# Causal attention and a mixture of experts on one core: half blocks of keys in 64 by 64 tiles, and six transfers let go one by one

## The chip, the core and the metric

The kernel runs on one core of a Trainium2 chip. The metric is the device time of one execution in microseconds; the median of the executions shown stands for the kernel.

## The reference

Eight batches of 576 tokens, eight heads of 64, then eight experts of which each token takes one:

```python
scores = q @ k.T / sqrt(64)                       # causal
cum = cumsum(max(s, 0))
scores = where(causal, -1e9, scores + min(cum_j - cum_i, 0))
x = softmax(scores) @ v                           # (B, H, S, D) -> (B, S, H*D)
logits, local = x @ w_gate, sigmoid(x @ w_local)
e = argmax(logits), or the previous token's e where local >= 0.5 and s > 0
out = softmax(logits)[e] * (relu(x @ w1[e]) @ w2[e])
```

All is in fp32. Each fp32 matmul of the program stands as two records (two passes) in the profile.

## The kernel before, in words

**Attention.** Two heads form a pair `n`; there are 32 pairs (four per batch), and two pairs form a slot `m`, so there are 16 slots. The bias of the reference is a factor of the key: `weigh(n)` multiplies the values of a pair, and a column of ones, by key weights `wk` into one of four buffers `vg`, so that the same product gives the sum of the softmax in a further column. A row of `vg` has 64 + 2 columns per head.

Keys lie in blocks of 128 (`c` = 0 to 3; `c` = 4, `NF`, holds the last 64, loaded as the last 128 keys with the first half weighted zero). Queries lie in blocks of 64 (`j` = 0 to 8).

`scores(n, u)` does one of four units: for every key block of `UNITS[u]` and for both heads one matmul, keys times queries, on tiles of 64 rows by 128 columns; the two heads lie on different rows, so they run at the same time. A unit fills a pair of banks of PSUM (`ps`, one bank per head). One exp on ACT (`L905`) takes the whole unit to `e`; then GpSimd zeroes what lies above the diagonal (`masked`, `L890`). The unit list decides how many columns are computed; for the 64 queries at the head of a 128-key block, the upper half of the keys is masked away again.

`values(n, j0, j1)` sums over the key blocks for each `j`: `e` is the stationary operand (128 keys by 64 queries), `vg` streams 66 columns (`L934`, tiles of 128 rows by 64 columns, the two heads side by side). It fills one bank for `j` below `NJA` = 6 and one for the rest; DVE takes the reciprocal of the sums (`L941`) and multiplies (`L942`) into `xb`. `turn` transposes for the gate product.

The order is written by hand; each engine runs its queue in that order. A slot is: four units of the first pair, four of the second, values of the first, values of the second, `turns` and `weigh` for later pairs. The pool `ps_s` is a ring of three bank pairs, of which each unit takes the next; `ps_o` has the two banks of the values. So a unit waits for the exp three units ahead of it. `plan(slot, place, f)` hangs the routing work on places in a slot (0 and 1 behind the scores of the two pairs, 3 and 4 behind their values, 5 at the end): in slots 4, 8, 12 and 15 the gate product (`product`, `L217`, on tiles of 128 by 32) and its `logits`; two slots later (6, 10, 14) `ranks` (`L301`, `L302`), `rows`, `gates`; then `scatter` of rows to a table in HBM by GpSimd (`L349`). Products and ranks also take bank pairs from the ring.

Transfers are issued by SP. A load that has to follow some work is held back by a copy of one element on ACT (`nc.scalar.copy(kb[0:1, 0:1], behind)`), which reads a result and writes into the tile to be loaded. Before, a slot has two such copies: values `v` of two pairs behind an exp (`L808`), and `k`, `q` of two pairs behind a value product (`L797`).

**Experts.** From 221.6 us on, units of up to 256 tokens go through two layers (`L608`, `L637`), 4 MB of weights for each unit. Nothing of it is changed.

Of the kernel before, what the change touches and what calls it, by code (L numbers as in the profile page):

```python
# [35 lines left out]
NJ = S // DH  # L36
NJA = 6
G1 = 2
REF = (127, 415)
UNITS = (((0, 0, 384, 0),), ((0, 384, S, 0), (3, 384, S, 192)), ((1, P, S, 0),), ((2, 256, S, 0), (NF, TS, S, 320)))  # L40
WIDTH = (384, 384, 448, 384)
GB = 2
# [8 lines left out]
BX = 3  # L51
FIRST = ((0, P, 0, 3 * P), (P, S, 3 * P, S))
CAP = N + DH
# [62 lines left out]
class Router:  # L116
# [104 lines left out]
    def logits(self, g, bs=range(GB)):  # L221
        v = self.nc.vector
        st = self.g[g]
        n, groups = self.columns(bs)
        lt = self.s("lt", [P, NJH, 2, WR])
        v.transpose(lt[:, :n].rearrange("p j q e -> p (j q e)"), st.pop("lp"))
        if "l" not in st:
            st["l"] = self.s("l", [P, NC, E + 1])
        l = st["l"]
        for c, (b, j, skip) in enumerate(groups):  # L230
            for r in range(2):
                v.tensor_copy(l[32 * r : 32 * r + 32, b * NJ + j + skip : b * NJ + j + n],
                              lt[32 * c : 32 * c + 32, skip:n, r, : E + 1])
        c = slice(bs[0] * NJ, bs[-1] * NJ + NJ)
        v.tensor_copy(l[DH:, c], l[:DH, c])

# [529 lines left out]
def attention(ctx, tc, q, k, v, s, wx, ident, recs, wend, router, experts):  # L766
# [9 lines left out]
    p_v = pool("p_v", NVA)  # L776
    p_e = pool("p_e", 2)
    p_x = experts.p_x
    p_x0 = pool("p_x0", 1)
# [6 lines left out]

    ins, vs, es, xs, xts = {}, {}, {}, {}, {}
    heads = [slice(DH * h, DH * h + DH) for h in range(2)]

    def load_qk(n, behind=None):  # L790

        if n >= NPAIR:
            return
        b, hp = divmod(n, HP)
        ins[n] = qb, kb = p_in.tile([P, S], F32, name="qb"), p_in.tile([P, S], F32, name="kb")
        if behind is not None:
            nc.scalar.copy(kb[0:1, 0:1], behind)  # L797
        for k0, k1, q0, q1 in FIRST if n == 0 else ((0, S, 0, S),):
            nc.sync.dma_start(kb[:, k0:k1], k[b][:, hp, k0:k1])  # L799
            nc.sync.dma_start(qb[:, q0:q1], q[b][:, hp, q0:q1])  # L800

# [21 lines left out]
    load_v(1)  # L823
    load_qk(2)
    load_v(2)
    load_qk(3)
    for n in range(3, NVA):
        load_v(n)
    router.projection(wx)
    wk = once.tile([P, NPAIR, G1 + NB, 2], F32, name="wk")  # L830
    nc.gpsimd.memset(wk[:TL, :, G1 + NF], 0.0)
    for t in vgs:
        nc.gpsimd.memset(t[..., VW - 1 : VW], 1.0)
        nc.gpsimd.memset(t[:TL, G1 + NF, :, VW - 1 : VW], 0.0)

# [18 lines left out]
    def key_weights():  # L854
        cps = banks("cps")[:, 0].rearrange("p (i n) -> p i n", n=B * H)
        i = 0
        for w, n in ((w1, G1), (w2, NB)):
            for c in range(n):
                a = min(c * P, S - P)
                tr(cps[:, i], w[:, a : a + P], ident[: B * H, : B * H])  # L860
                i += 1
        for i in range(G1 + NB):
            d = slice(TL if i == G1 + NF else 0, P)
            nc.vector.tensor_copy(wk[d, :, i, :].rearrange("p n h -> p h n"), cps[d, i].rearrange("p (h n) -> p h n", h=2))

# [22 lines left out]

    def masked(ap, n, base=0):
        nc.gpsimd.affine_select(out=ap, in_=ap, compare_op=Alu.is_ge, fill=0.0, base=base, pattern=n,  # L890
                                channel_multiplier=-1)

    def scores(n, u):
        if n >= NPAIR:
            return
        qb, kb = ins[n]
        if u == 0:
            es[n] = [p_e.tile([P, 2, w], F32, name=f"e{i}") for i, w in enumerate(WIDTH)]
        e = es[n][u]
        ps = banks("ps")[:, :, : WIDTH[u]]  # L900
        for c, a, z, at in UNITS[u]:
            key = min(c * P, S - P)
            for h, d in enumerate(heads):
                mm(ps[:, h, at : at + z - a], lhsT=kb[d, key : key + P], rhs=qb[d, a:z], start=True, stop=True)  # L904
        nc.scalar.activation(e, ps, Act.Exp, scale=scale)  # L905
        for c, a, z, at in UNITS[u]:
            m = min(P, z - a)
            if a < c * P + P:
                masked(e[:, :, at : at + m], [[0, 2], [1, m]], P - m)

# [12 lines left out]

    def values(n, j0, j1):
        b, hp = divmod(n, HP)
        if b not in xs:
            xs[b] = x_tile(b) if b < BX else p_x.tile([P, NJ, 2, XW], F32, name="xb")
        xb = xs[b]
        po = ps_o.tile([P, j1 - j0, VW], F32, name=f"po{j0}")
        for j in range(j0, j1):  # L930
            last = j // 2 if j < NJ - 1 else NF
            for c in range(last + 1):
                for h, d in enumerate(heads):
                    mm(po[d, j - j0, :], lhsT=weights_of(n, c, j, h),  # L934
                       rhs=vgs[n % NV][:, c if j < 2 * G1 else G1 + c, h, :],
                       start=(c == 0), stop=(c == last))

        def evacuate():
            m = j1 - j0
            rec = recs[:, n, j0:j1, :]  # L940
            nc.vector.reciprocal(rec, po[:, :, VW - 2 : VW])  # L941
            nc.vector.tensor_tensor(xb[:, j0:j1, :, 32 * hp : 32 * hp + 32], po[:, :, :DH].rearrange("p j (g i) -> p j g i", g=2),  # L942
                                    rec[:, :, 0].unsqueeze(2).unsqueeze(3).to_broadcast([P, m, 2, 32]), op=Alu.mult)

        return evacuate, po[0:1, 0, 0:1]

# [20 lines left out]
    for g in range(NG - 1):  # L967
        m = HP * GB // 2 * (g + 1)
        plan(m, 1, lambda g=g: router.product(g, of(g), banks))
        plan(m, 3, lambda g=g: router.logits(g))  # L970
        plan(m, 5, lambda g=g: (router.codes(g), router.turn1(g)))
        plan(m + 1, 1, lambda g=g: router.exps(g))
        plan(m + 1, 3, lambda g=g: router.turn2(g))
        plan(m + 2, 1, lambda g=g: router.ranks(g, banks))
        plan(m + 2, 3, lambda g=g: router.rows(g))
        plan(m + 2, 3, lambda g=g: router.gates(g, [xs[b] for b in range(g * GB, g * GB + GB)]))
        places = [(m + 2 + i, p) for i, ps in enumerate(STORES[g]) for p in ps]
        for c in range(NC):
            if c >= len(places):
                experts.puts.append(lambda after, g=g, c=c: router.scatter(g, c, after))  # L980
                continue
            i, p = places[c]
            after = {3: (2 * i, NJA), 4: (2 * i + 1, 0), 5: (2 * i + 1, NJA)}.get(p)
            after = after and recs[0:1, after[0], after[1], 0:1]
            plan(i, p, lambda g=g, c=c, after=after: router.scatter(g, c, after))
# [3 lines left out]
    plan(2, 3, range_ends)  # L989
    plan(m - 5, 3, lambda: router.assign_early(0))  # L990
    for i in range(4):
# [3 lines left out]
    plan(m - 1, 1, lambda: router.product(NG - 1, (xts[B - 2],), banks, (0,)))  # L995
    plan(m - 1, 3, lambda: router.logits(NG - 1, (0,)))

    def at(slot, place):
        for f in todo.pop((slot, place), ()):
            f()  # L1000

    for m in range(NPAIR // 2):
        pair = 2 * m, 2 * m + 1
        for n in pair:
            for u in range(len(UNITS)):
                if (n, u) == (0, 2):
                    key_exps()
                scores(n, u)
                if (n, u) == (0, 3):
                    key_weights()  # L1010
                    weigh(0)
                    weigh(1)
                if (n % 2, u) == (1, 1):
                    load_v(n - 1 + NVA, es[n][u][0:1, 0, 0:1])
                    load_v(n + NVA)
            at(m, n - 2 * m)
        for n in pair:
            values(n, 0, NJA)[0]()
            evacuate, done = values(n, NJA, NJ)
            if n % 2 == 0:  # L1020
                load_qk(n + NV, done)
                load_qk(n + 1 + NV)
            evacuate()
            at(m, 3 + n - 2 * m)
        last = m % HP == HP - 1
# [43 lines left out]
def attention_general(ctx, tc, q, k, v, s, w_gate, w_local, cum_d, x_d, ident, lg):  # L1069
# [24 lines left out]
    def load_batch(b):  # L1094
# [6 lines left out]
        nc.sync.dma_start(qb, q[b])  # L1101
        nc.sync.dma_start(kb, k[b])
        for hp in range(HP):
            hs = slice(2 * hp, 2 * hp + 2)
            nc.sync.dma_start(vb[:, :, hs], v[b, hp][:, :NF])
            nc.sync.dma_start(vl[:, hs], v[b, hp][TL:, NF])
        ins[b] = qb, kb, vb, vl
# [500 lines left out]
```

## Time and profile before

| | |
|---|---|
| median of 3 executions | 729.42 us (729.3 to 730.54) |
| the profiled execution, own time | 748.85 us |
| its span | 747.1 us |
| granted TensorE clock | 0.994 |
| attention, up to the first expert matmul | 221.6 us |
| experts | from there to the end |

The profile is of one execution, and its own time is above that of the others; durations and gaps of single steps are read from it, and differences are set against its own order of events. A matmul's end is modelled, so a step is read from start to start: the time from one matmul to the next that follows it on the same tile. PEld is the weight load of TensorE, which overlaps with its matmuls. "Idle before" is time of the engine in front of the named group, and the releaser is what ended it.

### The profile page before, as it was taken

The page shows a single profiled execution, that of the slowest core. Times are in us where ns is not written, and L with a number is a line of the kernel's source. Part 1 is how long each engine was busy: PE and PEld are TensorE (multiplying, and loading weights), DVE is VectorE, ACT ScalarE, POOL GpSimd, SP SyncE. Part 2 cuts the span into 40 slices and gives each one's busy share as a digit, 9 for nine tenths or more (in the row PEclk, how much of TensorE's full clock was granted, in tenths as well). Part 3 has the DMA queues.
Part 4 walks back from the last instruction along what each step waited for, and adds up shares of the span by engine and source line. Part 5 has one row for each costly group of instructions (what it writes and reads, how often), then busy time and mean ns, then how long its engine had stood idle before and what let it go on. Part 6 is the DMA issues. An engine that isn't in the chain of part 4 may idle for free.

```text
span 747.1 us, 16231 instructions
## 1 busy us (share of the span) xinstructions
PE 729.2 (98%) x6537; PEld 504.9 (68%) x6537; DVE 257.7 (34%) x714; ACT 166.0 (22%) x355; POOL 206.7 (28%) x453
## 2 busy tenths in 40 slices
PE   8999999999998999999999999999999999999996
PEld 7888878878876567567567365637644676673675
DVE  4656668677756383101100411041132001104110
ACT  4645454354331011011011010201010111110111
POOL 3543367577574245350100011010101001000100
PEclk9999999999998999999999999999999999999999
DMA  8464455665629996598555979996999965976700
GB/s 303 145 189 149 152 191 165 201 199 172 188 81 382 341 396 218 208 424 240 203 190 169 375 258 396 342 382 237 425 334 390 423 215 214 307 268 239 269 15 32
DMA packets 57205, 187.28 MB, mean 251 GB/s; under 512 B 11837, under 2 KB 32061, under 8 KB 49568
## 3 DMA queue, kind: packets, MB, share of 16 engines
q1 hardware_dynamic: 50224, 165.91, 62.3%
q0 software_dynamic: 6800, 20.09, 7.0%
q8 instruction: 53, 0.87, 0.5%
q14 instruction: 32, 0.26, 0.1%
q10 hardware_dynamic: 96, 0.15, 0.1%
HBM read 165.50 MB, written 20.75 MB: 249 GB/s over the span
## 4 chain that ended last, share of the span: by engine, by line
PE 95%; issue 2%; POOL 1%; DVE 1%; DMA 1%; ACT 0%; SPq 0%; POOLq 0%; ACTq 0%
PE yp L637 34%; PE hp L608 31%; PE po L934 13%; PE ps L904 11%; PE hp L599 4%; PE lp L217 2%; DMA qb<-in_q_dram 1%; POOL table L349 0%; ACT e L905 0%; PE pos L301 0%; POOL e L890 0%; PE pos L302 0%; DVE xb L942 0%; SPq L799 0%; POOL out_dram L641 0%
## 5 line engine op out<-in xcount | busy, mean ns | idle before, releaser
L637 PE MATMUL yp<-w2b,hT 128*128 128x512 f32 (+4 forms) x768 | 258.4, 584 | 0.0
L608 PE MATMUL hp<-xT,w1b 128*128 128x256 f32 (+2 forms) x1216 | 232.0, 352 | 0.0
L608 PEld LDWEIGHTS hp<-xT,w1b 128*128 128x128 f32 x1216 | 207.7, 192 | 30.0 <-issue 7.8
L637 PEld LDWEIGHTS yp<-w2b,hT 128*128 128x128 f32 (+3 forms) x768 | 109.9, 167 | 138.4 <-issue 136.1
L641 POOL DMA_INDIRECT out_dram<-y,gi x37 | 36.4, 984 | 412.3 <-DVE y L639 380.0
L610 ACT ACTIVATE hT<-hp 128x256 f32<-128x256 f32 (+2 forms) x152 | 53.6, 353 | 430.4 <-PE hp L608 417.2
L639 DVE TENSOR_SCALAR y<-yp,gi 128x512 f32<-128x512 f32 (+2 forms) x38 | 27.8, 731 | 299.8 <-PE yp L637 293.4
L934 PE MATMUL po<-vg,e 128*64 128x66 f32 x3200 | 105.2, 223 | 6.9 <-issue 5.6
L934 PEld LDWEIGHTS po<-vg,e 128*64 128x64 f32 x3200 | 98.7, 138 | 13.1 <-issue 10.5
L905 ACT ACTIVATE e<-ps 128x768 f32<-128x768 f32 (+1 forms) x128 | 97.0, 837 | 46.5 <-PE ps L904 45.8
L904 PE MATMUL ps<-qb,kb 64*128 64x192 f32 (+4 forms) x768 | 94.7, 398 | 0.6 <-ACT e L905 0.3
L904 PEld LDWEIGHTS ps<-qb,kb 64*128 64x128 f32 x768 | 64.7, 186 | 29.6 <-ACT e L905 14.9
L890 POOL TENSOR_SCALAR_AFFINE_SELECT e<-e 128x256 f32<-128x256 f32 (+1 forms) x160 | 67.2, 444 | 50.3 <-ACT e L905 49.3
L349 POOL DMA_INDIRECT table<-xb,idx x54 | 54.5, 1009 | 19.6 <-issue 16.8
L619 DVE STREAM_TRANSPOSE hT<-hs 32x256 f32<-32x256 f32 x64 | 27.9, 436 | 78.9 <-ACT hs L601 78.1
L884 DVE TENSOR_TENSOR vg<-va,wk 128x256 f32<-128x256 f32 x64 | 41.5, 714 | 0.0
L941 DVE RECIPROCAL recs<-po 128x12 f32<-128x12 f32 x64 | 13.5, 211 | 64.0 <-PE po L934 45.2
L599 PE MATMUL hp<-w1b,xT 128*32 128x512 f32 (+1 forms) x224 | 28.3, 594 | 0.0
L578 DVE STREAM_TRANSPOSE xT<-xq 128x1024 f32<-128x1024 f32 (+1 forms) x23 | 23.6, 1028 | 11.8 <-DMA xq<-table 11.7
L942 DVE TENSOR_TENSOR xb<-po,recs 128x384 f32<-128x384 f32 (+1 forms) x48 | 22.0, 458 | 2.2 <-POOL xb L325 0.6
L599 PEld LDWEIGHTS hp<-w1b,xT 128*32 128x32 f32 (+1 forms) x224 | 8.1, 114 | 17.8 <-issue 17.8
L953 DVE STREAM_TRANSPOSE xt<-xb 128x576 f32<-128x576 f32 x24 | 17.1, 751 | 0.0
(254 smaller groups left out, 202.6 us busy)
## 6 DMA issues: line engine op xcount, KB each, us to landing
w2b<-in_w_dram SPq DMA_DIRECT2D x30, 2048.0 KB
w1b<-in_w_dram SPq DMA_DIRECT2D x29, 2048.0 KB
va<-in_v_dram SPq DMA_DIRECT2D x32, 320.0 KB
kb<-in_k_dram SPq DMA_DIRECT2D x31, 288.0 KB
qb<-in_q_dram SPq DMA_DIRECT2D x31, 288.0 KB
xq<-table SPq DMA_DIRECT2D x56, 130.0 KB
w1b<-in_w_dram SPq DMA_DIRECT2D x4, 512.0 KB
xq<-table SPq DMA_DIRECT2D x20, 65.0 KB
```

The source lines that it names most:

```text
L349: put = self.nc.gpsimd.indirect_dma_start(out=self.halves, in_=src, element_offset=0, in_offset=None, out_offset=bass.IndirectOffsetOnAxis ...
L599: mm(ps[d, :], lhsT=xT[:, k, d], rhs=self.ws[l][0][:, k, c * 512 : c * 512 + 512], start=(k == 0), stop=(k == DK - 1))
L608: mm(ps[:, :w], lhsT=self.ws[ls[0]][0][:, k, c * P : c * P + P], rhs=xT[:, k, :w], start=(k == 0), stop=(k == DK - 1))
L610: nc.scalar.activation(self.hT[u][:, c, :w], ps[:, :w], Act.Relu)
L619: self.nc.vector.transpose(hT[32 * a : 32 * a + 32, :, 32 * r : 32 * r + 32], hs[32 * r : 32 * r + 32].rearrange("p (c i) -> p c i", i=P)[ ...
L637: mm(ps[d, :], lhsT=hT[:, k, n * P + d.start : n * P + d.stop], rhs=self.ws[l][1][:, k, f : f + w], start=(k == 0), stop=(k == FK - 1))
L641: put = nc.gpsimd.indirect_dma_start(out=self.out[:, :], out_offset=bass.IndirectOffsetOnAxis(ap=gi.bitcast(I32)[:m, n, 0:1], axis=0), in_ ...
L884: nc.vector.tensor_tensor(vg[:, to].rearrange("p c h e -> p (c h) e")[:, :, :DH], va[:, :c].rearrange("p c h e -> p (c h) e"), wk[:, n, to ...
L890: nc.gpsimd.affine_select(out=ap, in_=ap, compare_op=Alu.is_ge, fill=0.0, base=base, pattern=n, channel_multiplier=-1)
L904: mm(ps[:, h, at : at + z - a], lhsT=kb[d, key : key + P], rhs=qb[d, a:z], start=True, stop=True)
L905: nc.scalar.activation(e, ps, Act.Exp, scale=scale)
L934: mm(po[d, j - j0, :], lhsT=weights_of(n, c, j, h), rhs=vgs[n % NV][:, c if j < 2 * G1 else G1 + c, h, :], start=(c == 0), stop=(c == last))
```

## The change

1. **Key order.** The blocks of 64 keys are stored in the order 8, 0, 1, 2, 3, 5, 4, 7, 6 (`BLOCKS`). A 128-key block then starts at the second 64 in storage; the last 64 keys lie at the front.
2. **Three units instead of four.** For each 128-key block the 64 queries at its diagonal that see only half of its keys are left out of `scores`: 512, 384 + 64 and 256 + 128 columns per head, 1344 instead of 1600.
3. **`scores_halves(m)`** computes what was left out: the diagonal blocks 0, 2, 4 and 6 of both pairs of a slot, as 64 by 64 tiles, 16 matmuls of 64 columns in one pair of banks `ph`, one exp of 512 columns and two masks. Blocks 0 and 2 go to one half of the partitions, 4 and 6 to the other. It runs one slot ahead: in slot `m` the halves of slot `m + 1` are done, directly behind the scores (slot 0 does its own too).
4. **`values_halves(n)`** multiplies them with `vg` on 64 by 64 tiles (8 matmuls per pair) into the same sums; `values` has 21 instead of 25 products per head. `NJA` becomes 4, so that the two key halves of a step go to different banks.
5. **Banks.** The values of a slot's second pair (`pb`) and `ph` take bank pairs from the ring of three; the first pair keeps `po`.
6. **Order in a slot:** scores a, scores b, half values a, half scores of the next slot, half values b, values a with evacuation, values b with evacuation.
7. **Transfers.** Six per slot (two `v`, two `k`, two `q`) are let go each behind its own copy, at points named in `POINTS`: behind an exp (`e00` is unit 0 of the first pair), behind the last exp and the half scores (`h`), behind the evacuations of the first pair (`x0`, `x1`). Slot 0 lets go four, slot 1 eight; the last two slots none. Two loads of `v` fewer are issued at the start.
8. **Routing.** Work of place 3 moves to place 1, and the copies of `logits` go from DVE to ACT where both batches are done at once (slots 4, 8, 12).

The core of the diff:

```diff
-UNITS = (((0, 0, 384, 0),), ((0, 384, S, 0), (3, 384, S, 192)), ((1, P, S, 0),), ((2, 256, S, 0), (NF, TS, S, 320)))
-WIDTH = (384, 384, 448, 384)
+BLOCKS = (8, 0, 1, 2, 3, 5, 4, 7, 6)
+UNITS = (((0, DH, S, 0),), ((1, 3 * DH, S, DH), (NF, TS, S, 0)), ((2, 5 * DH, S, 0), (3, 7 * DH, S, 256)))
+WIDTH = (512, 448, 384)
+HALVES = ((0, 4), (2, 6))
+POINTS = {0: ("h", "x0", "x1", "y0"), 1: ("e00", "e10", "e20", "e01", "e11", "h", "x0", "x1"), 2: ("e00", "e20", "e11", "h", "x0", "x1")}
...
+        copy = self.nc.scalar.copy if len(bs) == GB else v.tensor_copy
...
-        for k0, k1, q0, q1 in FIRST if n == 0 else ((0, S, 0, S),):
-            nc.sync.dma_start(kb[:, k0:k1], k[b][:, hp, k0:k1])
-            nc.sync.dma_start(qb[:, q0:q1], q[b][:, hp, q0:q1])
+        todo = [(kb, k, 0, S), (qb, q, 0, S)] if n else [(kb, k, 0, DH + P), (qb, q, 0, FIRST), (qb, q, FIRST, S), (kb, k, DH + P, S)]
+        for to, src, a, z in todo:
+            nc.sync.dma_start(to[:, a:z], src[b][:, hp, a:z])
...
+            for to, of in (heads[:2],) if c == NF else (heads, heads[::-1]) if c in TURNED else ((d, d),):
+                nc.vector.tensor_copy(wk[to, :, i, :].rearrange("p n h -> p h n"),
+                                      cps[of, i].rearrange("p (h n) -> p h n", h=2))
...
+    def scores_halves(m, ps):
+        eh[m] = p_eh.tile([P, 2, 2, len(HALVES), DH], F32, name="eh")
+        ps = ps[:, :, : 4 * DH]
+        for i in range(2):
+            qb, kb = ins[2 * m + i]
+            for t, blocks in enumerate(HALVES):
+                for side, x in zip(heads, blocks):
+                    at = (2 * i + t) * DH
+                    key = BLOCKS.index(x) * DH
+                    for h, d in enumerate(heads):
+                        mm(ps[side, h, at : at + DH], lhsT=kb[d, key : key + DH], rhs=qb[d, x * DH : x * DH + DH],
+                           start=True, stop=True)
+        nc.scalar.activation(eh[m].rearrange("p h n t i -> p h (n t i)"), ps, Act.Exp, scale=scale)
...
+    def values_halves(n, po, first):
+        e = eh[n // 2][:, :, n % 2]
+        for t, blocks in enumerate(HALVES):
+            for part, (side, j) in enumerate(zip(heads, blocks)):
+                for h, d in enumerate(heads):
+                    mm(po[part][d, j - PARTS[part][0], :], lhsT=e[side, h, t],
+                       rhs=vgs[n % NV][side, j // 2 + (G1 if part else 0), h, :],
+                       start=(first > 0 and t == 0), stop=(first == 0 and t == 1))
...
-        for n in pair:
-            values(n, 0, NJA)[0]()
-            evacuate, done = values(n, NJA, NJ)
-            if n % 2 == 0:
-                load_qk(n + NV, done)
-                load_qk(n + 1 + NV)
-            evacuate()
-            at(m, 3 + n - 2 * m)
+        a, b = pair
+        po = room(a)
+        if m == 0:
+            for i in range(2):
+                values(a, po, i, True, False)
+        values_halves(a, po, m)
+        halves = banks("ph") if b + 1 < NPAIR else None
+        to = room(b)
+        scores_halves(m + 1, halves)
+        values_halves(b, to, True)
+        let_go("h", es[b][2][0:1, 0, P : P + 1])
+        for i in range(2):
+            if m:
+                values(a, po, i, False, True)
+            evacuate(a, po, i)
+            let_go(f"x{i}", recs[0:1, a, PARTS[i][0], 0:1])
+        at(m, 3)
+        for i in range(2):
+            values(b, to, i, False, True)
+            evacuate(b, to, i)
+            let_go(f"y{i}", recs[0:1, b, PARTS[i][0], 0:1])
+        at(m, 4)
```

`room(n)` gives `po` for the first pair and `banks("pb")` for the second. `let_go(place, behind)` takes the next of the slot's parts, if the place is one of its points: a one-element ACT copy of `behind` into the tile, then SP's transfer.

## The prediction

> **What bounds the kernel now.** I read the page's busy shares first, then its chain of work that ended last.
>
> ```profile
> PE 729.2 (98%) x6537; PEld 504.9 (68%) x6537; DVE 257.7 (34%) x714; ACT 166.0 (22%) x355; POOL 206.7 (28%) x453
> PE 95%; issue 2%; POOL 1%; DVE 1%; DMA 1%; ACT 0%; SPq 0%; POOLq 0%; ACTq 0%
> ```
>
> TensorE is busy 98% of the span and carries 95% of the chain. The chain in order of time shows the attention stage as slots of two steps without a hole between them:
>
> ```profile
> 43.64 5.76 PE ps L904 x48
> 49.40 5.98 PE po L934 x200
> 55.39 5.76 PE ps L904 x48
> ...
> 210.74 1.46 PE lp L217 x64
> ```
>
> So a slot is 5.76 + 5.98 = 11.74 us of pure TensorE. Behind attention (from 221.6 us on) TensorE runs through the experts without waiting, so a microsecond won in a slot is won at the end. A share would have misled here: ACT is busy 22% of the span, but the table by stretch has it at 6.6 us of this 11.74 us slot, and all eight exps fall into the score half and a little behind it:
>
> ```profile
> 43.57:55.31 11.74, 11.74 (x252) 9.97 (x248) 6.38 (x14) 6.61 (x12) 4.11 (x10) 1.00 0.57 171
> L905 ACT ACTIVATE e<-ps 128x768 f32<-128x768 f32 x96 | 73.0, 812 | 46.5 <-PE ps L904 45.8 <-issue 0.7
> L905 ACT ACTIVATE e<-ps 128x896 f32<-128x896 f32 x32 | 29.2, 914 | 0.0
> ```
>
> Columns of the first line: stretch, its length, then busy us of PE, PEld, DVE, ACT, POOL. The ACT timeline of one slot gives its pace:
>
> ```profile
> 59.24 1.53 ACT L905 ACTIVATE e<-ps 128x768 f32<-128x768 f32 x2
> 60.80 0.19 ACT L808 COPY va<-e 1x1 f32<-1x1 f32 x1
> 60.90 0.90 ACT L905 ACTIVATE e<-ps 128x896 f32<-128x896 f32 x1
> ```
>
> Two exps together take 1.53 us, so the second began at 59.93, 0.69 behind the first. The one-element copy that lets a transfer go reads the exp just issued and waits for its end; the exp behind it starts 0.97 after the one before. **Such a copy costs ACT 0.28 us.**
>
> **What the Trainium skill says.** "TensorEngine Tiling (Array Packing)", Tiling Modes: 64x64 gives four tiles, tiles load and multiply independently, and a change of mode drains the array. The trace agrees on the drain: from the last score matmul to the first value matmul it is 202 ns where a 64-column step takes 56, so 146; back it is 93 plus 107 of bare weight load. It has two- and four-tile steps (64\*128, 128\*64, 128\*32) but no 64\*64 one. The same page, Gotcha 1, wants row tiles in different PSUM banks; the new code does that (heads to banks in the scores, the two parts in the values). "ScalarE: Activation LUTs", What ACT_TABLE_LOAD costs: 186 ns + 0.833 ns a column, overlapping by 93. The rows of 812 and 914 ns sit 10 to 20 ns under it.
>
> **The change part by part**, by start times of matmuls in the clean slot. A step (one pass of all tiles that run together) takes 0.833 ns a column + 3: 163 ns for 192, 376 for 448, 323 for 384, 58.3 for the 66 of the values.
>
> *Removed, scores.* A pair's steps before: 2 x (323 + 163 + 163 + 376 + 270) + 168 (the 64-column piece, one of its two steps waiting for a 128-column weight load of 107) = 2.76 us. After: 2 x (429 + 323 + 216 + 109) + 168 = 2.32. Twice 0.44: 0.87 us a slot.
>
> *Removed, values.* 25 products a head become 21: 100 steps a slot become 84; 16 x 58.3 ns = 0.93.
>
> *Added, half blocks.* 16 score and 16 value matmuls a slot on 64\*64 tiles, each in two passes: 8 + 8 four-tile steps. **Their duration is the unknown.** Lower bound: streaming, 56 and 58. Upper: two tiles at a time, 112 and 117. For the lower speak the L217 row (64 records in 1.46 us with the change of mode; inside, a four-tile step of 96 columns every 83 ns, starts 7 ns apart, so issue isn't the limit) and two row tiles with 107 ns weight loads stepping in 112, hence loading together. I take the lower: 8 x 56 + 8 x 58.3 = 0.92.
>
> *One more change of mode*: 0.15. Without waits: 0.87 + 0.93 - 0.92 - 0.15 = **0.73 us off a slot**.
>
> *What ACT takes back.* Six transfers now have six copies instead of two; three (e00, e20, e11) stand between exps. And ph and pb take two pairs of banks from the ring of three: the built program has ph wait for the exp of b0, and pb for that of b1 (a, b: the slot's pairs; 0 to 2: units). Exps follow at 0.92 (1024 columns, extrapolated), 0.81 and 0.69; one starts 0.27 after its scores' last column (the slot that begins at 55.31: columns end at 56.07, exp at 56.34); TensorE resumes 0.05 after an exp (exp ends at 182.55, scores go on at 182.60). From the slot's first matmul, ACT: a0 1.24; copy; a1 2.44; a2 3.25; copy; b0 4.22; b1 5.14, ending 6.05. TensorE: b1's scores, ready at 3.29, wait for a1's exp until 3.40; scores end 4.86; drain; halves of a 5.01 to 5.24; ph waits until 5.29, ends 5.74; halves of b wait until 6.10, plus 0.05 of bare weight load. Then 0.24 + 0.15 + 4.90 + 0.09: 11.53. Waits 0.52, so **0.21 off a plain slot** (2, 3, 5, 7, 9, 11, 13): 1.5 us. What was TensorE's becomes a wait for ACT; behind the wait for pb on TensorE's queue stand all values of the slot, and behind those their evacuation and the next slot, so nothing makes it up.
>
> *Other slots.* 1: five copies among the exps, b1 ends at 6.66: 0.35 lost. 4, 8, 12: the gate product (2.3 us) covers the wait for pb: 0.62 each, 1.9. 6, 10: the rank product takes a bank pair, so pb waits for b2's exp (7.04) behind only 0.7 us of cover: 0.1 lost together. 14: no transfers left: 0.7 won. 15: no half scores either: 1.2 won. 0: 0.1 lost: its scores end earlier, but the values can't start before `weigh` (before: DVE from 10.74, values at 12.77; now nine wk copies instead of seven ahead of it, 0.26 each), so from about 12.8 it is 4.90 + 0.47 + 0.45 + 2 x 0.15 = 6.1 instead of 5.98. Sum: 1.5 - 0.35 + 1.9 - 0.1 + 0.7 + 1.2 - 0.1 = **4.75 us won**.
>
> *At nothing.* POOL: masks per slot go from 10 to 8 over the same 2304 columns; its busy 4.1 to 7.6 us a slot leave room, and the half masks have most of a slot until they are read. If POOL fell behind by over 3 us, values would wait. DVE: four evacuations a slot as before; pb must be free for the third unit of the next slot, 1.8 us in, and the two instructions (0.2 + 0.5) follow the last matmul at once; the logits' nine copies go to ACT in slots 4, 8, 12, behind all exps that TensorE needs there. SP: as many q, k, v issues; the last q goes at about 9.8 us, takes some 4 (four such landed 4.9 us after the last issue at 54.6) and is read at 16.8; if it came later, ph would wait for the difference. The first load brings 192 columns of keys instead of 128, 32 KB more, ahead of an unchanged 384 of queries. The copies at h, x0, x1 queue behind the exps and have only `weigh`'s copies behind them.
>
> The profiled execution took 748.85 us (span 747.1), 19.4 above the median of 729.42. Gaps put down to "issue" among the value matmuls (some 12 us) are part of that. I keep them out on both sides and take the difference from the median: 729.42 - 4.75 = 724.7 (a profiled execution after: some 744).
>
> **The rivals.** *Half-block steps run two tiles at a time* (slower). Nothing in the trace shows 64\*64 concurrency. Each slot gets 0.93 more; a plain slot's waits for ph and pb vanish inside it: 4.86 + 0.15 + 0.47 + 0.90 + 0.47 + 0.15 + 4.90 + 0.09 = 11.99, 0.25 lost; the seven plain slots lose 1.7, slot 1 0.6, the three with gate products 0.9, 6 and 10 0.7, 14 0.2, 0 1.0; 15 wins 0.7. Together 4.4 slower: 733.8. It decides from a step of about 88 ns on (the two ends, linearly). *ACT holds nobody up* (the copies overlap): 14 slots at 0.73, 1.2 and -0.1: 11.3 won, 718.1. For it: the chain of before has ACT at 0%; against: fifth to eighth units there had only about 0.2 us to spare, and now ACT gets 0.6 us more of copies ahead of pb's release while TensorE gets 0.9 us less of scores. *The gain is eaten by small things* (a dearer 64\*64 drain, 0.3 more a slot; late q; 272 matmul records a slot instead of 248, so more of the "issue" gaps): 16 x 0.3 is the whole sum, about 729.4.
>
> **How the numbers follow.** A measurement here can tell about 0.2% (1.5 us). ACT-bound as worked out: 0.54, 724.7, own range 721 to 728. ACT free: 0.14. Two tiles at a time: 0.20. Eaten up: 0.12. Faster: 0.52 + 0.14 = 0.66; within 0.2%: 0.10; slower: 0.20 and a share of the last case, 0.24. The range, 717.5 to 732.5, cuts off the lower edge of the second case and the greater part of the third.
>
> **What would show it.** In a plain slot: half-block steps 56 to 58 ns apart (88 refutes the gain); L904's successor about 4.7 us of scores; ACT named as releaser of the first half-value matmul of b, for some 0.4 us; value step 4.9. An 11.5 us slot is the forecast, 11.0 the second case, 12.0 the slower one. Wrong altogether if a plain slot shows waits for POOL or DMA.

## The result and the profile after

The changed kernel takes 725.61 us (median of 6 executions, 724.57 to 727.9) against 729.61 us of the kernel before on the same chip (6 executions, 729.3 to 730.54). The ratio is 0.9945, interval [0.9933, 0.9957]: 4.0 us or 0.55% faster, 0.9 us from the forecast of 724.7. Its profiled execution took 725.8 us (span 724.1), so this profile, unlike that of before (748.85 us), stands for the median.

Busy shares and the shares of the chain, on the page of the changed kernel:

```profile
PE 711.5 (98%) x6925; PEld 489.2 (68%) x6925; DVE 252.0 (35%) x689; ACT 173.7 (24%) x423; POOL 203.4 (28%) x421
PE 96%; ACT 1%; issue 1%; DMA 1%; DVE 0%; POOL 0%; SPq 0%; POOLq 0%; ACTq 0%
```

TensorE has more instructions (6925 for 6537) and is busy for less time (711.5 us for 729.2); it still carries the chain. ACT, at 0% before, is now named with 1%. The TensorE timeline of a plain slot of the changed kernel (start us, extent us, group; a group's extent runs to its last modelled end, so read the starts):

```profile
43.44 5.14 PE L916 MATMUL ps<-qb,kb 64*128 64x512 f32 x40
48.51 0.46 PE L987 MATMUL po<-vg,eh 64*64 64x66 f32 x16
48.79 0.64 PE L938 MATMUL ph<-qb,kb 64*64 64x64 f32 x32
49.41 0.46 PE L987 MATMUL pb<-vg,eh 64*64 64x66 f32 x16
49.80 2.67 PE L975 MATMUL po<-vg,e 128*64 128x66 f32 x84
52.30 2.62 PE L975 MATMUL pb<-vg,e 128*64 128x66 f32 x84
54.85 0.70 PE L916 MATMUL ps<-qb,kb 64*128 64x512 f32 x2
```

From start to start: scores 5.07, half values of a 0.28, half scores 0.62, half values of b 0.39, values 5.05; together 11.41 where before had 11.74. Inside the half scores the eight four-tile steps follow each other in 58 ns, and the four tiles of one step start 6 to 7 ns apart: the last step starts at 49.20 and would be done at 49.25, yet `pb` starts at 49.41. The ACT timeline of the same slot shows what it waits for:

```profile
44.67 1.02 ACT L917 ACTIVATE e<-ps 128x1024 f32<-128x1024 f32 x1 [0.90 <-PE ps L916]
45.73 0.19 ACT L815 COPY va<-e 1x1 f32<-1x1 f32 x1
45.83 1.59 ACT L917 ACTIVATE e<-ps 128x896 f32<-128x896 f32 x2
47.45 0.19 ACT L815 COPY va<-e 1x1 f32<-1x1 f32 x1
47.55 1.81 ACT L917 ACTIVATE e<-ps 128x1024 f32<-128x1024 f32 x2
```

The exp of b1 is the second of the last line. It ends at 49.36, and `pb` starts 0.05 later. The profile itself names no releaser there, because the modelled end of the half scores (48.79 + 0.64 = 49.43) lies behind that start; that ACT is waited for follows from the times, and from the runs below. ACT works without a hole from 44.67 on, so every copy ahead of this exp moves it.

**The gain depends on the chip.** The table has all comparisons, each with the kernel before on the same chip. In the first comparison (whose chip is not on record, so it may be C) and on chip C before takes 729.6 to 730.0 us, on three others 746.4 to 747.0. On the first kind the gain came again (chip C), on the second kind it did not (A and B). Each chip was met on one occasion only, so what belongs to the chip and what to the occasion can't be told apart. Experiments are therefore compared within a chip.

| chip | kernel | us | ratio to before [95%] |
|---|---|---|---|
| first | before | 729.61 | |
| first | changed | 725.61 | 0.9945 [0.9933, 0.9957] |
| A | before | 746.53 | |
| A | values first | 746.38 | 1.0004 [0.9985, 1.0024] |
| A | copies late | 746.95 | 1.0003 [0.9987, 1.0018] |
| A | two copies | 746.91 | 1.0013 [1.0001, 1.0025] |
| A | ring order (the changed kernel in effect) | 749.74 | 1.0062 [1.0037, 1.0087] |
| B | before | 746.39 | |
| B | before, second series | 745.87 | 0.9994 [0.9982, 1.0007] |
| B | changed | 748.33 | 1.0037 [1.0025, 1.0049] |
| B | two tiles | 750.04 | 1.0044 [1.0024, 1.0064] |
| B | before with six copies | 755.37 | 1.0118 [1.0098, 1.0138] |
| C | before | 729.96 | |
| C | changed | 725.86 | 0.9939 [0.9924, 0.9954] |
| C | copies late | 725.52 | 0.9937 [0.9921, 0.9953] |
| C | scatters moved | 729.61 | 0.9995 [0.9983, 1.0007] |
| D | before | 747.02 | |
| D | late but the last | 745.62 | 0.9983 [0.9970, 0.9996] |

### The profile page after: what moved, and what is told of

Same layout as the page of the kernel before. It is cut to its first block, busy times and chain, and to the rows that moved or that the text cites. A ratio compares the mean times of both kernels' runs of the same rounds, so it can differ in the third digit from the quotient of the medians.

```text
span 724.1 us, 17075 instructions
## 1 busy us (share of the span) xinstructions
PE 711.5 (98%) x6925; PEld 489.2 (68%) x6925; DVE 252.0 (35%) x689; ACT 173.7 (24%) x423; POOL 203.4 (28%) x421
## 4 chain that ended last, share of the span: by engine, by line
PE 96%; ACT 1%; issue 1%; DMA 1%; DVE 0%; POOL 0%; SPq 0%; POOLq 0%; ACTq 0%
PE yp L643 35%; PE hp L614 31%; PE ps L916 10%; PE po L975 6%; PE pb L975 6%; PE hp L605 4%; PE lp L222 1%; ACT e L917 1%; PE ph L938 1%; PE pb L987 1%; PE po L987 1%; DMA kb<-in_k_dram 1%; DVE wk L872 0%; PE pos L307 0%; SPq L807 0%
## 5 line engine op out<-in xcount | busy, mean ns | idle before, releaser
L917 ACT ACTIVATE e<-ps 128x1024 f32<-128x1024 f32 (+2 forms) x96 | 83.3, 906 | 37.4 <-PE ps L916 37.4
L916 PE MATMUL ps<-qb,kb 64*128 64x64 f32 (+5 forms) x644 | 82.7, 407 | 1.7 <-DMA kb<-in_k_dram 1.0
L916 PEld LDWEIGHTS ps<-qb,kb 64*128 64x128 f32 x644 | 52.3, 187 | 30.2 <-ACT e L917 10.7
L900 POOL TENSOR_SCALAR_AFFINE_SELECT e<-e 128x128 f32<-128x128 f32 (+2 forms) x96 | 43.2, 458 | 49.5 <-ACT e L917 48.7
L975 PE MATMUL pb<-vg,e 128*64 128x66 f32 x1344 | 43.5, 222 | 2.3 <-issue 2.2
L975 PEld LDWEIGHTS pb<-vg,e 128*64 128x64 f32 x1344 | 41.5, 138 | 3.1 <-issue 3.0
L975 PE MATMUL po<-vg,e 128*64 128x66 f32 x1344 | 42.8, 223 | 0.0
L975 PEld LDWEIGHTS po<-vg,e 128*64 128x64 f32 x1344 | 40.6, 138 | 1.2
L893 DVE TENSOR_TENSOR vg<-va,wk 128x256 f32<-128x256 f32 x64 | 38.8, 670 | 0.0
L900 POOL TENSOR_SCALAR_AFFINE_SELECT eh<-eh 64x512 f32<-64x512 f32 (+1 forms) x32 | 21.1, 660 | 11.5 <-ACT qb L1064 7.5
```

The lines of the kernel that those rows point to most:

```text
L893: nc.vector.tensor_tensor(vg[:, to].rearrange("p c h e -> p (c h) e")[:, :, :DH], va[:, :c].rearrange("p c h e -> p (c h) e"), wk[:, n, to ...
L917: nc.scalar.activation(e[:, :, : WIDTH[u]], ps, Act.Exp, scale=scale)
L975: of = mm(po[part][d, j - a, :], lhsT=weights_of(n, c, j, h), rhs=vgs[n % NV][:, c if j < 2 * G1 else G1 + c, h, :], start=(first and i == ...
```

## The experiments

**Theory A** is the prediction's: four-tile steps run at full speed, and ACT, slowed by the copies, takes part of the gain back. Rivals: two tiles at a time; the ring of banks rather than the copies; late transfers; and, once chips A and B were seen, gaps of TensorE that are no part of a slot's steps: idle time for which the profile shows no wait and which it puts down to "issue".

### Values of a ahead of the half blocks

```diff
-        if m == 0:
-            for i in range(2):
-                values(a, po, i, True, False)
-        values_halves(a, po, m)
+        for i in range(2):
+            values(a, po, i, True, False)
+        values_halves(a, po, 0)
...
-            if m:
-                values(a, po, i, False, True)
```

> The values of the slot's first pair stand ahead of the half-block work (as slot 0 of the changed kernel already has it); nothing else differs, and the number of changes of mode is the same. Theory A (in a plain slot TensorE waits for ACT about 0.14 us before the half values of b, plus 0.05 of bare weight load, because pb takes the bank pair of b1): the 2.5 us of values cover that wait; a plain slot goes from 11.42 to about 11.23, slots 6 and 10 win 0.3, in all 2 to 3 us under the changed kernel, some 723. The 0.10 before the scores of b1 stays. Theory B (TensorE's steps and changes of mode are all there is, no wait to cover): same as the changed kernel, 725.6 within 0.7.

Its TensorE timeline in a slot without gaps:

```profile
68.64 5.13 PE L916 MATMUL ps<-qb,kb 64*128 64x512 f32 x40
73.70 2.67 PE L975 MATMUL po<-vg,e 128*64 128x66 f32 x84
76.30 0.46 PE L987 MATMUL po<-vg,eh 64*64 64x66 f32 x16
76.58 0.65 PE L938 MATMUL ph<-qb,kb 64*64 64x64 f32 x32
77.05 0.41 PE L987 MATMUL pb<-vg,eh 64*64 64x66 f32 x16
77.39 2.43 PE L975 MATMUL pb<-vg,e 128*64 128x66 f32 x74
```

The wait for b1's exp is gone: half scores 0.47 instead of 0.62, half values of b 0.34 instead of 0.39. But the order needs one more change of mode, which I had overlooked, and the values take 2.60 twice, 5.20 instead of 5.05. A wait of 0.20 was exchanged for a drain of 0.15. The kernel is nevertheless 3.4 us faster than the changed kernel on this chip (749.74, below). The slots without gaps don't show where: a plain slot wins 0.05 (11.36), slot 6 0.16 (12.18), slot 4 loses 0.15 (13.78). In its profile the gaps, to which I come back, are 9.9 us against 17.3; whether they are the reason is not shown.

### The copies behind the last exp, and only two copies

```diff
+        if m > 3:
+            parts = parts[2:] + parts[:2]
+            points = "e21", "h", "x0", "x1", "y0", "y1"
```

The first edit moves the copies, the second leaves two of them:

```diff
+        if m > 3:
+            vq = [lambda x: load_v(2 * m + NV, x), lambda x: load_v(2 * m + 1 + NV)], [
+                lambda x: load_qk(2 * m + NV, x), lambda x: load_qk(2 * m + 1 + NV)]
+            parts = [lambda x, fs=fs: [f(x) for f in fs] for fs in vq] if 2 * m + NV < NPAIR else []
+            points = "e11", "x1"
```

> From slot 4 on none of the six copies stands between exps of a slot: k, q, k, q, then the two v are let go at e21, h, x0, x1, y0, y1. Theory A: without three copies of 0.2 to 0.28 us ahead of b1's exp, that exp ends about 0.7 us earlier; both waits of a plain slot (0.10 before b1's scores, 0.19 with weight load before the half values of b) go: 0.29 less in slots 5, 7, 9, 11, 13, 0.1 in 8 and 12, 0.4 in 6 and 10: about 2.5 us under the changed kernel, 723. Theory B: no change (725.6). Rival C (transfers let go so late arrive late): a wait of half scores for q or k, or of weigh for v, and slower than the changed kernel.

> The half blocks stay, the transfers go back to two copies from slot 4 on: both v behind the exp of b1 (e11), both k and q of two pairs behind the evacuation of the first pair (x1). Theory A: no copy ahead of b1's exp, so as in the run before it: 0.29 less in a plain slot, some 723, if the four q and k (1.15 MB, let go at about 9 us in the slot, read 7.5 us later) land in time; in the kernel before, four such took until 4.9 us after the last issue, so they should be just in time. Rival C (the spreading is what the half scores need): half scores of the next slot wait for q by a microsecond or more, 726 to 735.

The slot without gaps, with the copies late:

```profile
68.41 5.03 PE L916 MATMUL ps<-qb,kb 64*128 64x512 f32 x40
73.37 0.46 PE L987 MATMUL po<-vg,eh 64*64 64x66 f32 x16
73.66 0.64 PE L938 MATMUL ph<-qb,kb 64*64 64x64 f32 x32
74.12 0.41 PE L987 MATMUL pb<-vg,eh 64*64 64x66 f32 x16
74.47 2.67 PE L975 MATMUL po<-vg,e 128*64 128x66 f32 x84
76.97 2.62 PE L975 MATMUL pb<-vg,e 128*64 128x66 f32 x84
79.52 0.70 PE L916 MATMUL ps<-qb,kb 64*128 64x512 f32 x2
```

Scores 4.96 instead of 5.07, half scores 0.46 instead of 0.62, half values of b 0.34 instead of 0.39: 11.11 for the slot, and 11.10 with two copies (68.69 to 79.79 in its timeline). All three waits vanish with the copies, and the ring is as before: **the copies on ACT cost 0.30 us a slot, the ring nothing once they are gone.** On this chip the two are 2.8 us faster than the changed kernel, and within 0.4 us of the kernel before. With two copies the half blocks stand alone: they win 0.64 of the 11.74 us slot, and letting go the transfers one by one only takes from it.

### The order in which the ring is taken

```diff
-        halves = banks("ph") if b + 1 < NPAIR else None
         to = room(b)
+        halves = banks("ph") if b + 1 < NPAIR else None
```

> Only the order in which two bank pairs are taken from the ring is swapped: pb before ph. Theory A: now ph takes the pair of b1, and the half scores, which TensorE reaches first, wait until b1's exp ends (about 5.97 us in the slot instead of starting at 5.35); pb is free at once. The half values of b start near 6.45 instead of 5.97: 0.45 more in a plain slot, less where a gate product stands ahead: about 5 us slower than the changed kernel, 730 to 731. Theory B (the ring isn't what TensorE waits for): no change, 725.6.

It tested nothing: a pair of banks is evidently taken from the ring at its first use, not where it is named, so the built program has the same waits as the changed kernel and plain slots of 11.41, with the same 0.62 for the half scores. It serves as the changed kernel on chip A: 749.74 us, 1.0062 of before.

### The changed kernel and the kernel before, on another chip

> The changed kernel once more, to stand beside the others of this group on the same chip. On the chip of the group before, the kernel before took 746.5 instead of 729.6, and all traces there have gaps among the value matmuls in which nothing is waited for (issue), most of them from slot 7 on. Theory I (the gaps belong to the chip and the run, and grow with the number of TensorE instructions a slot): where the kernel before is near 729.6 the changed one is 4 us faster, as first measured; where it is near 746 the gain is gone or turned into a loss of up to 0.6%. Theory J (the first comparison was a lucky one): slower here whatever the kernel before takes.

> The kernel before, for a second profile of it. Theory I: its gaps put down to issue among the value matmuls follow the run, not the kernel: near 729.6 us there are few (under 4 us in all), near 746 some 12 us, as in the first profile of it (748.85).

The loss is real: 748.33 against 746.39 us (and 745.87 in the second series of before). Its plain slots without gaps are as long as ever (68.58 to 80.00: 11.42), so the loss is not in the steps that the prediction added up. What TensorE waited for, over the whole execution (us in total, times, longest), in the changed kernel on chip B:

```profile
PE pb L975 <- issue: 5.4, 16, 0.5
PE lp L222 <- issue: 2.9, 4, 1.1
PE po L975 <- issue: 2.4, 8, 0.4
PE pb L987 <- issue: 1.2, 4, 0.4
PE ps L916 <- ACT e L917: 0.8, 2, 0.5
```

and in before on chip B:

```profile
PE po L934 <- issue: 5.9, 16, 0.9
PE lp L217 <- issue: 1.9, 4, 0.5
```

Read from start to start among the value and half-block matmuls of attention (what is above a step of 58 ns, where over 130 ns), the gaps are 16.4 us in the changed kernel and 12.7 in before. They lie in slots with scatters, 7 to 13 and 15, mostly in clusters of 0.4 and twice 0.6 us with five or so matmuls between. So the changed kernel has 3.7 us more of them in these two profiles. Slots 1 to 6, which have no scatters, take 72.6 us in the changed kernel and 74.4 in before; slots 7 to 15, which have them, take 130.1 and 128.2. That is the right direction and not the full account: a gain of some 5 us in the slots less 3.7 would still be a gain, and the profiled executions themselves took 747.2 and 749.16, the reverse of the medians.

The POOL and TensorE timelines of the changed kernel on chip B show when a cluster begins:

```profile
102.70 1.00 POOL L355 DMA_INDIRECT table<-w1b,idx  x1 [0.16 <-issue]
104.04 0.98 POOL L355 DMA_INDIRECT table<-w1b,idx  x1 [0.16 <-issue]
103.94 0.35 PE L975 MATMUL pb<-vg,e 128*64 128x66 f32 x4 [0.15 <-issue]
104.67 0.39 PE L975 MATMUL pb<-vg,e 128*64 128x66 f32 x5 [0.38 <-issue]
105.41 0.69 PE L975 MATMUL pb<-vg,e 128*64 128x66 f32 x15 [0.36 <-issue]
```

The first scatter ends at 103.70; the last matmul ahead of the cluster starts at 103.57, the next one at 103.94. Counted over attention: 31 of the 43 scatters end while half blocks, values or a gate product run, and with 24 of them TensorE has a gap of over 0.25 us (from one record's start to the next, weight loads included) that begins within 0.25 us of the scatter's end. With all ends shifted by 1 us to either side it is 8 of 24 and 10 of 29. Of the 12 that end during scores none has one. In before on chip B it is 15 of 26, and none of the 17 that end during scores; in the changed kernel on chip C (below), 1 of 25. The other runs on A and D agree with B (24 of 31 for the ring order, 18 of 30 for late but the last; the least is 7 of 21, for values first). **So on this kind of chip the gaps come with the ends of scatters, and the changed kernel has more scatters that end outside the scores.** What in a scatter does it, and why not on chip C, stays open; no run removed the scatters on such a chip.

### Two tiles at a time

```diff
-        for i in range(2):
-            qb, kb = ins[2 * m + i]
-            for t, blocks in enumerate(HALVES):
-                for side, x in zip(heads, blocks):
+        for s in range(2):
+            for i in range(2):
+                qb, kb = ins[2 * m + i]
+                for t, blocks in enumerate(HALVES):
+                    side, x = heads[s], blocks[s]
...
-        for t, blocks in enumerate(HALVES):
-            for part, (side, j) in enumerate(zip(heads, blocks)):
+        for part in range(2):
+            for t, blocks in enumerate(HALVES):
+                side, j = heads[part], blocks[part]
```

One half of the partitions is written out after the other:

> The half blocks in another order: all of one key half first, then the other, so that neighbouring matmuls repeat the same two tiles and a step has two tiles instead of four. Theory A (a four-tile step lasts 58 ns, as long as one with two): 16 steps more a slot, 0.93 us, of which a plain slot hides 0.14 in its wait for ACT: 0.8 more in a plain slot, 11 to 13 us over the changed kernel in all, which puts it above the kernel before. Theory B (the tiles' parallel work brings nothing, the gain comes from fewer columns alone): within 1 us of the changed kernel.

It was to make the steps slow, and hardly did: 1.7 us over the changed kernel, where some 12 were expected. The timeline says why:

```profile
44.42 5.13 PE L916 MATMUL ps<-qb,kb 64*128 64x512 f32 x40
49.49 0.48 PE L989 MATMUL po<-vg,eh 64*64 64x66 f32 x16
49.77 0.83 PE L939 MATMUL ph<-qb,kb 64*64 64x64 f32 x28
50.39 0.27 PE L989 MATMUL pb<-vg,eh 64*64 64x66 f32 x1
50.43 0.28 PE L939 MATMUL ph<-qb,kb 64*64 64x64 f32 x4
50.50 0.51 PE L989 MATMUL pb<-vg,eh 64*64 64x66 f32 x15
50.94 2.67 PE L976 MATMUL po<-vg,e 128*64 128x66 f32 x84
```

A matmul of `pb` starts at 50.39, ahead of four of `ph` that stand before it in the program. **A tile goes on with its own queue while the others are still busy**, so the two halves of the partitions overlap although they are written one after the other. The Trainium skill, "TensorEngine Tiling (Array Packing)", Key Properties, says that different tiles load weights and multiply in parallel; the trace agrees, and goes further, in that they also overtake. The slot takes 11.57 instead of 11.42. The dear case of that rival could not be brought about in this way; what refutes it is the 58 ns step.

### Six copies in the kernel before

```diff
+                ex = es[n][u][0:1, 0, P + 2 : P + 3]
+                if (n % 2, u) == ((0, 1) if m else (1, 0)):
+                    load_v(2 * m + NVA, ex)
+                if (n % 2, u) == ((0, 2) if m else (1, 1)):
+                    load_v(2 * m + 1 + NVA, ex)
                 if (n % 2, u) == (1, 1):
-                    load_v(n - 1 + NVA, es[n][u][0:1, 0, 0:1])
-                    load_v(n + NVA)
+                    load_part(2 * m + NV, 1, ex)
+                if (n % 2, u) == (1, 3):
+                    load_part(2 * m + NV, 0, ex)
...
-                load_qk(n + NV, done)
-                load_qk(n + 1 + NV)
...
+                load_part(2 * m + 1 + NV, 1, recs[0:1, n, 0, 0:1])
+                load_part(2 * m + 1 + NV, 0, recs[0:1, n, NJA, 0:1])
```

Two values, a key and a query go behind four exps, the other key and query behind the evacuations of the first pair.

> The kernel before with the second half of the change alone: six copies a slot, three of them among the eight exps (behind units 1 and 2 of the first pair and unit 1 of the second), one behind the last exp, two behind the evacuation of the first pair. Theory A (a copy that reads the exp just issued holds ACT up 0.2 to 0.28 us, and TensorE has about 0.2 us to spare there): the third unit of the second pair waits for ACT, about 0.4 us in 13 slots, some 5 us slower than the kernel before. Theory B (copies overlap with exps): no change.

9.0 us slower than before. Its TensorE timeline has a plain slot of 12.18 us instead of 11.74, and among its waits stands ACT:

```profile
73.16 6.27 PE L913 MATMUL ps<-qb,kb 64*128 64x384 f32 x48
79.36 6.05 PE L943 MATMUL po<-vg,e 128*64 128x66 f32 x200
85.34 0.92 PE L913 MATMUL ps<-qb,kb 64*128 64x384 f32 x4
```

```profile
PE ps L913 <- ACT e L914: 4.0, 8, 1.2
```

Scores take 6.20 instead of 5.76, the values 5.98 as before. Letting go the transfers one by one, put alone into the kernel before, costs 0.44 a slot, which in 14 slots is some 6 of the 9.0 us. Some slots took more (7.5 us of scores at 113.81, where ACT itself stood idle for 1.31 us without a wait that the profile shows), which the 0.44 does not explain.

### A third chip: the change, the copies late, the scatters moved

> The changed kernel once more, to see on a third chip whether its gain depends on the gaps. Theory: where before takes about 729.6 (hardly any gaps) the ratio is 0.9945 as in the comparison, 725.6; where before takes about 746 (13 us of gaps in its attention) it is 1.003, 748.5. Rival, the first comparison was an accident: 1.003 in both cases.

> The changed kernel with all six copies of a slot behind the last exp, again, beside the changed kernel. By the waits found so far it is 2.8 us faster than the changed kernel on any chip (0.30 in each of some ten slots, less where other work covers the wait): 722.8 where before takes 729.6, about 746 where before takes 746.4. Rival: the later transfers run late on this chip and it is within 1 us of the changed kernel.

> The changed kernel with the scatters of the routing moved: none in slots 6 to 8, six in each of slots 9 to 11, nine in 12 and 13 (before: 1, 5, 5, 5, 4, 5, 5, 6 in slots 6 to 13); their number is the same. It asks what the gaps among the value matmuls are tied to ('issue' in the profile; in two kernels' runs so far 13 and 17 us of attention, from slot 7 on). Theory A, they come with the scatters: slots 7 and 8 lose theirs (slot 7 from 13.7 to 11.4 us, slot 8 from 16.4 to 13.7), slots 9 to 13 keep or gain, the sum stays near 17 us, the time within 3 us of the changed kernel's. Rival B, they come with TensorE's own instructions, whatever else runs: slots 7 and 8 keep 2.3 and 2.7 us of gaps. Should before run at about 729.5 on this chip, as it did in the comparison, the gaps are small everywhere and the run tells only what the move costs (theory: under 1 us).

*The changed kernel again:* 0.9939, 725.86 us against 729.96, as in the first comparison. TensorE's waits over the execution:

```profile
PE pb L975 <- issue: 3.2, 3, 1.3
PE ps L916 <- ACT e L917: 0.8, 2, 0.5
PE po L975 <- issue: 0.6, 1, 0.6
```

Five gaps of 4.8 us together, of up to 1.5 us each, and none of the clusters of chip B. So the gain goes with the gaps: 0.994 where the changed kernel has few, 1.004 to 1.006 where it has many. The gaps are not all that sets the two kinds of chip apart: the experts, which the change leaves alone, take 519.5 us in this profile and 523.1 in that of chip B (attention 206.6 and 222.4).

*Copies late:* 725.52, no gain over the changed kernel, against the forecast of 722.8. The slots had won what was forecast (11.11 for slot 5, 11.10 for slot 7), but in the profiled execution (728.8 us, the longest of its six, the others 724.0 to 727.2) slot 15 lost more than that:

```profile
189.15 1.94 PE L916 MATMUL ps<-qb,kb 64*128 64x512 f32 x12 [0.31 <-DVE base L318]
194.16 6.26 PE L916 MATMUL ps<-qb,kb 64*128 64x256 f32 x28 [3.07 <-DVE xb L997]
```

Its scores take 11.2 us instead of 5.0: they wait for DVE to empty `pb`. The chain followed back from there, and the DVE timeline, show what DVE itself waited for:

```profile
176.76 9.25 DMA va<-in_v_dram
```

```profile
186.11 1.16 DVE L893 TENSOR_TENSOR vg<-va,wk 128x256 f32<-128x256 f32 x2 [6.26 <-DMA va<-in_v_dram]
```

The last values of slot 13 were let go at its end, behind two 512 KB weight loads on SP's queue, took 9.25 us, and held up `weigh` and, behind it on DVE's queue, the routing and the evacuations of slot 14. On chip A the same kernel has 5.24 us of scores in slot 15; that the gaps gave the transfer its time there is a guess. Nor is it shown that the other five executions stalled too, so why the median gained nothing is open.

*Scatters moved:* the edit is one constant (none in slots 6 to 8; six each in 9 to 11; nine each in 12 and 13). It should have told whether gaps go with scatters, but on this chip slots 7 and 8 have no gaps in either kernel, so **this run can't tell**; the timelines of chip B above do. What it showed instead is a price: 3.8 us, where under 1 was expected. In slot 14 the values of the first pair waited for a mask on POOL, the longest line of its waits:

```profile
PE po L975 <- POOL e L900: 3.4, 2, 3.2
PE pb L975 <- POOL e L900: 0.8, 1, 0.8
```

Nine scatters of 1.0 us, each with its small copy, fill POOL's queue, and the masks stand behind them.

### Copies late, but not in slot 13

```diff
+        if 3 < m < 13:
+            parts = parts[2:] + parts[:2]
+            points = "e21", "h", "x0", "x1", "y0", "y1"
```

> The changed kernel with all copies behind the last exp in slots 4 to 12, but slot 13 as in the changed kernel. Theory: the six copies of slot 13 behind the last exp let the last values go so late, behind 512 KB weight loads, that their transfer took 9.25 us and DVE, queued behind them, freed the banks of slot 15 some 6 us late; with slot 13 as it was, slot 15's scores take 5.0 us again instead of 11.2, and the waits for ACT stay away in slots 4 to 12: 2.9 us off the changed kernel (0.22 in each of slots 4, 8, 12, 0.30 in 5, 7, 9, 11, 0.52 in 6, 10). That is 722.7 where before takes 729.7 (ratio 0.990), and about 745.5 where before takes 746.4 (0.999). Rival: the stall of slot 15 was chance, or another late transfer takes its place (slot 14), and it is 725.5 again, ratio 0.994.

It met a chip of the second kind, and there is faster than before: 0.9983 [0.9970, 0.9996]. The forecast for such a chip was 745.5 and a ratio of 0.999; the measured time is 745.62, with a kernel before that takes 747.02 instead of 746.4. Slots 5 and 6 start at 70.46 and 81.56, 11.10 apart. Slot 15 has 4.96 us of scores, but as copies late did not stall on such a chip either, this run does not show that the stall of chip C is cured; the 722.7 forecast there was not tried.

## Why the prediction was right

| step | predicted | measured |
|---|---|---|
| four-tile steps, 64 and 66 columns | 56 and 58.3 ns | 58 and 58.3 |
| plain slot without waits | 11.01 us | 11.10 to 11.11 (copies late, two copies) |
| scores of b1 wait for ACT | 0.10 | 0.11 (5.07 less 4.96) |
| wait for `ph` | 0.05 | none seen |
| wait for `pb` and the bare weight load | 0.36 + 0.05 | 0.15 + 0.05 |
| plain slot | 11.53 | 11.41 |
| slot 1 against before | 0.35 lost | 0.22 lost (11.96, chip C), 0.08 of it a gap |
| slots 4, 8, 12, each | 0.62 won | 0.43 (14.06 to 13.63) |
| slots 6, 10, each | 0.05 lost | 0.12 won (12.46 to 12.34) |
| slot 14 | 0.7 won | 0.64 (12.46 to 11.94, 0.12 of it a gap) |
| slot 15 | 1.2 won | 1.06 (13.20 to 12.14) |
| slot 0, from the start of its values | 0.1 lost | 0.31 lost (7.01 with a gap of 1.03, to 6.29) |

**The mechanism held, link by link**: full-speed four-tile steps, and ACT as the new wait at `pb`, shown by removing the copies (0.30 back) and by adding them to the kernel before (0.44 lost a slot).

**Terms that were mis-sized.** The wait for `pb`: 0.15, not 0.36. ACT was faster than assumed, as exp to exp with a copy between took 1.16 for 1024 columns (taken as 1.20) and 0.91 for 768 (taken as 0.97), so b1's exp ended 5.92 us into the slot instead of 6.05; and TensorE was a little later, as the slot without waits is 0.09 longer than worked out, a second error that offset the first. In slots 4, 8 and 12 the gate product does cover the wait for `pb`, but 0.21 us ahead of the product remains (5.17 us from the scores at 54.85 to the product, 4.96 with two copies). The prediction's four waits also add up to 0.56, not to its 0.52.

**The sum.** The measured slots, gaps left out, give 7 x 0.33 - 0.14 + 3 x 0.43 + 2 x 0.12 + 0.64 + 1.06 - 0.31 = 5.1 us, the medians 4.0 and 4.1. Part of what lies between may be the start of slot 0's values (13.24 us in this profile, 12.77 in that of before; 13.64 and 13.39 in those of chips C and B). The rest was not located: the changed kernel has 3 to 5 us of gaps in its profiles on these chips, and no profile shows before at 729.6.

**Where it was not right in general, and lucky.** Gaps were "kept out on both sides". On the chip of the comparison and on C that is good to about 1 us; on A and B it fails. That the comparison met the first kind was luck: the prediction had no reason for it, and its own profile of before, at 748.85 us, has the marks of the second kind (12.4 us of gaps; with 17 of 26 scatters that end outside the scores one begins at the end). The rival "eaten by small things" named the means, 272 matmul records a slot instead of 248 and so more gaps, and put it at 729.4, no change; on A and B it came to a loss of 1.9 to 3.2 us. That the gaps tell the two kinds of chip apart, and that on the second kind they come with the ends of scatters, is shown. That more instructions make more of them is not, and nor is it that they make up the whole loss.

## What to carry to other kernels

A one-element copy that lets a transfer go is not free on an engine whose results free the banks that TensorE needs next: put it behind the last such result, and then check whether the transfer, now later, stands behind a long one. Cost the engine's order instruction by instruction, not its share of the span: ACT, at 24%, held TensorE up in each plain slot. Where TensorE idles without a wait that the profile shows, lay its gaps beside the other engines' timelines. A gain of half a per cent that adds TensorE instructions wants its comparison on more than one chip.

## What the runs showed of the hardware

- 64 by 64 tiles in fp32 run four at a time, a step (one pass) of 64 or 66 columns every 58 ns; a tile overtakes the program order of the others (50.39 before 50.43 us in the run with two tiles).
- One more change of mode between half blocks and values made the values 0.15 us longer (5.20 us a slot with the values of a ahead, 5.05 otherwise).
- A one-element copy of an exp's result, put behind that exp on ACT, delays the next exp by 0.22 to 0.28 us (0.91 and 0.97 from start to start behind 768 columns, 0.69 without it).
- The same kernel before takes 729.6 to 730.0 us in two series and 746.4 to 747.0 on three other chips, at a granted clock of 0.99 or more in the profiles. On chip B gaps of TensorE begin at the end of 24 of the 31 scatters that end outside the scores, on chip C of 1 of 25.
